# A third buffer for high and low parts, a spread change from the cosine half to the sine half, and one transposition for maxima and sums

## The chip, the cores and the metric

One core of a Trainium2 chip. The metric is the device time of one launch in microseconds, the median of several runs.

## What is computed

Two branches of the same input x (2048 rows of 512, fp32) are mixed by a gate of each row:

```
g = sigmoid((x * gate_w).sum(-1))
a = x @ Wd_re.T ;  b = x @ Wd_im.T              # DFT along the 512 columns
A = Ws_re @ a - Ws_im @ b                       # DFT along the 2048 rows, real part
q, k, v = x @ wqkv                              # 32 heads of 16
p = softmax(mask(q @ k.T / 4))                  # a row sees itself and the 255 rows before it
B = (p @ v) @ wo
out = g * A + (1 - g) * B
```

## The kernel before

**Precision.** Every dense product is made of three matmuls: each fp32 operand is split into a rounded high part and the rest, the low part (`split`, lines 77 to 81, from SBUF; `split_psum`, lines 83 to 88, from PSUM), and `TERMS` (line 223) lists high by high, high by low and low by high.

**Two streams in one order.** TensorE's order is written by hand. The loop at the end of the kernel (from line 710) goes over 128 attention blocks n (4 groups of heads by 32 blocks of 64 rows). In block n it makes four score matmuls (`s_pair`, L324), for which VectorE takes the row maxima (L326, into `nm`) and ScalarE the exponentials' sums (L329, into `l`). For block k = n - 20 it makes four transposed score matmuls (`t_pair`, L393), whose operands hold the negated maxima in four extra rows, and every third block it multiplies probabilities by v (`pv`, L420). Between these, `fill` pulls 3 to 3.6 dense matmuls per quarter block from the generator `dense`, which yields after each matmul. The order of VectorE, ScalarE, GpSimd and SyncE (SP) is decided by a scheduler from simulated times and from what waits for what; `behind(...)` puts an instruction behind the last marked one of an engine. All large transfers but one kind are issued from SP's queue, in order.

**The dense stream** has these stages. First q, k (`qk_proj`, L243) and v (`v_proj`, L265). The q and k blocks leave PSUM through `qk_evict`: ScalarE writes the high part and VectorE the low part of a tile `hl` (4 KB per partition, two buffers), and SP stores it in `qk_scr`. `ring_load` fetches it back into `ring`, from which `make_pad` (L307, L309) builds the padded stationary operands; one quarter of a ring (512 rows) is loaded when its last readers are done, a few blocks ahead of the first `make_pad` that needs it. Then b and a (`ab_proj`, L265): b goes through the same `hl` tiles into `ab_scr`; of a, 12 of the 16 chunks are written straight into tiles `big` (16 buffers), and 4 go through `hl` and `ab_scr`. Beside it the gate is computed (`gate`, L208, with `gwb`, the gate's weights, as a constant tile).

Then comes the joint over the 2048 rows, in two halves: half 0 with the cosine matrix and a, half 1 with the sine matrix and b. A block `tb` (16 per half) accumulates 16 chunks by 3 terms, 48 matmuls (L451), in one PSUM buffer of `ps_d` (two). The matrix comes in pieces of 8 chunks (`c_pieces`), 512 KB each, which VectorE splits. Half 0 stores its blocks, times g, in `r_scr[0]` (`store_r`, L567). Half 1 loads them, adds its own (`add_r`, L588) and stores the sum in `r_scr[1]`; once attention is done, the blocks are combined with the output projection (`wo_block`, L638, L640).

At the change of halves all 16 tiles `big` have to go from a to b. `c_pair` does it: the last two blocks of half 0 run side by side, the second four chunks (`BEHIND`) behind the first, and when both have used a chunk, its tile is loaded with the b chunk. The first two blocks of half 1 run as a pair too.

**Maxima and sums.** Eight blocks after another (16 times in all) the 32 columns of maxima and the 32 columns of sums are transposed on TensorE: `m_rows` (L336) negates and splits the maxima (L339, L340) and stores them in `m_scr`, `l_rows` (L352) takes the reciprocals (L350) before and a copy (L354) after and stores them in `l_scr`. Both come one after the other in the order. `m_ring` fetches the maxima into the ring from ScalarE's queue (L346) one block later. `pv` loads the reciprocals into `rl` (one buffer of the pool `at`) and multiplies (L430).

**Small tiles.** The pool `ev` has five buffers of 2 KB per partition, for v, `store_r`, `add_r` and the output projection.

Of the kernel before, what the change touches and what calls it, by code (L numbers as in the profile page):

```python
# [7 lines left out]
F32 = mybir.dt.float32  # L8
# [19 lines left out]
BEHIND = 4  # L28
# [4 lines left out]
def fnet_window_mix(ctx: ExitStack, tc: tile.TileContext, xT, x, wqk, wv, wr, wi, cr, ci, wo, gw, out):  # L33
# [19 lines left out]
    r_scr = [[dram.tile([P, D], F32, name=f"r_scr{i}_{c}") for c in range(16)] for i in range(2)]  # L53
# [140 lines left out]
    gwb = const.tile([P, D], F32, name="gwb")  # L194
# [3 lines left out]
    def gate_load(j):  # L198
        if j == 0:
            with behind("sp"):  # L200
                ld(gwb, bass.AP(tensor=gw.tensor, offset=gw.offset, ap=[[0, P], [1, D]]))
        GX[j] = st.tile([P, 1024], F32, name="raw", bufs=2)
        for c in range(2):
            ld(GX[j][:, HALVES[c]], x[2 * j + c])

    def gate(tb):
        t = GX[tb // 2][:, HALVES[tb % 2]]
        nc.vector.scalar_tensor_tensor(t, t, 1.0, gwb, op0=OP.mult, op1=OP.mult,  # L208
                                       accum_out=gl[:, tb:tb + 1])
# [74 lines left out]
    def ab_proj(i, sb, w, dst=None):  # L284
        ps = ps_d.tile([P, 512], F32, name="dab", tag="d")
        yield from row_proj(sb, w, ps)
        if dst is None:
            hl = ev.tile([P, 2, 512], F32R, name="hl", bufs=2)
# [43 lines left out]
    def m_rows(u):  # L332
        U = u % 4
        nm = ML[u][0]
        pt = ps_a.tile([P, 512], F32, name="s", tag="st")
        nc.tensor.matmul(pt[:32, :P], nm, ident, start=True, stop=True)  # L336
# [4 lines left out]
        ld(m_scr[u].rearrange("x p (j r) -> (p j) x r", r=64), f(hl[:]).rearrange("c a h r -> c (a h) r"))  # L341

# [4 lines left out]

    def l_rows(u):
        l = ML.pop(u)[1]
        nc.vector.reciprocal(l, l)  # L350
        pt = ps_a.tile([P, 512], F32, name="s", tag="st")
        nc.tensor.matmul(pt[:32, :P], l, ident, start=True, stop=True)  # L352
        lt = at.tile([32, P], F32, name="lt", bufs=1)
        nc.vector.tensor_copy(lt, pt[:32, :P])  # L354
        for a in range(2):
            ls = l_scr[u]
            ld(bass.AP(tensor=ls.tensor, offset=ls.offset + a * 512, ap=[[1024, NP], [64, 8], [1, 64]]),
               lt[:, 64 * a:64 * a + 64])
# [47 lines left out]
    def pv(n):  # L406
# [41 lines left out]
    def c_chunk(w, i, ab, ps):  # L448
        s8 = i % 8
        for a, b in TERMS:  # L450
            nc.tensor.matmul(ps, w[a][:, s8 * 128:(s8 + 1) * 128], ab[SC[i]][:, b],  # L451
                             start=i == 0 and a + b == 0, stop=i == 15 and a == 1)
            if i < 15 or a == 0:
                yield

    def c_block(get, half, tb, ab, done):
        ps = ps_d.tile([P, 512], F32, name="dc", tag="d")
        for i in range(16):
            if i % 8 == 0:
                w = get((half, tb * 2 + i // 8))  # L460
            yield from c_chunk(w, i, ab, ps)
# [3 lines left out]
    def c_pair(get, half, tb, ab, done, last=False):  # L465
        ps = [ps_d.tile([P, 512], F32, name="dc", tag="d") for _ in range(2)]
        w = [None, None]
        for i in range(16 + BEHIND):
            for h in range(2):
                k = i - BEHIND * h  # L470
                if 0 <= k < 16:
                    if k % 8 == 0:
                        w[h] = get((half, 2 * (tb + h) + k // 8))
                    yield from c_chunk(w[h], k, ab, ps[h])
                    if last and h:
                        nxt[SC[k]] = load_ab(1, SC[k])
                    if k == 15:
                        done(tb + h, ps[h])
                        yield
# [13 lines left out]
    def dense():  # L493
# [71 lines left out]
        def store_r(tb, ps):  # L565
# [4 lines left out]
        get = c_pieces([*((0, k) for k in (*range(28), 28, 30, 29, 31)),  # L570
                        *((1, k) for k in (0, 2, 1, 3, *range(4, 32)))])
# [6 lines left out]
        mixed = {}  # L578

        def add_r(tb, ps):  # L580
            r = mixed.pop(tb, None)
            late_r = r is not None
            if not late_r:
                r = ev.tile([P, 512], F32, name="ev")
                ld(r, r_scr[0][tb])
# [9 lines left out]
        yield from c_pair(get, 1, 0, ab, add_r)  # L595
        for tb in range(2, 16):
# [33 lines left out]
    def wo_block(tb, half):  # L630
        o = O.pop(tb)
        r = ev.tile([P, 512], F32, name="ev")
        ld(r, r_scr[half][tb])
# [41 lines left out]
    maxima = sent = 0  # L675
    need(("qk", 0, 0))
# [3 lines left out]
    for n in range(N + LAG + 2):  # L680
# [16 lines left out]
        for p in range(NP):  # L697
# [68 lines left out]
```

## Time and profile before

| | |
|---|---|
| median of 3 runs | 873.6 us (870.97 to 875.23) |
| profiled execution | 873.98 us, of which the span from first to last instruction is 872.2 us |
| TensorE busy | 860.1 us, 5192 matmul instructions |
| VectorE, ScalarE, GpSimd busy | 601.9, 581.4, 387.8 us |
| moved by DMA | 153.70 MB, mean 176 GB/s |

The profile is of one execution. "PE" is TensorE's matmuls, "PEld" its weight loads, DVE is VectorE, ACT ScalarE, POOL GpSimd, SP SyncE; "SPq" is an instruction that SP's queue issues. L451 is line 451 of the kernel before. Matmuls are pipelined, so the duration of one is longer than the step from its start to the next one's start; a step is read from two start times. A name such as dc<-big,hi is the tile written and those read.

### The profile page before, as it was taken

What the parts mean: (1) busy time and instruction counts of PE and PEld (TensorE: products, weight loads), DVE (VectorE), ACT (ScalarE), POOL (GpSimd) and SP (SyncE); (2) the same over time, 40 slices, a digit from 0 to 9 for tenths busy, and PEclk for the clock granted to TensorE, in tenths of its full rate; (3) what the DMA queues carried; (4) which work ended last, traced back from release to release, by engine and by line L of the source; (5) the groups of instructions that cost most, each with busy time, mean ns of one, the idle gap of its engine ahead of it and who ended that gap; (6) DMA issues with size and microseconds to landing.
All of it is one profiled execution on the core that took longest, in us unless ns stands there. A gap on an engine that the chain in (4) does not pass through costs nothing.

```text
span 872.2 us, 17214 instructions
## 1 busy us (share of the span) xinstructions
PE 860.1 (99%) x5192; PEld 693.5 (80%) x5192; DVE 601.9 (69%) x1966; ACT 581.4 (67%) x1793; POOL 387.8 (44%) x1067
## 2 busy tenths in 40 slices
PE   9999999999999999999999999999899999999998
PEld 7888778787878778788787887878678787788886
DVE  4588986667879987778787777878585444564431
ACT  5488799888988888788788877878676454111110
POOL 9100154445536746656465666554466665200000
PEclk9999999999999999999999999999999999999999
DMA  7865686465758537634355353589644332376541
GB/s 244 286 218 172 217 253 191 161 207 174 235 171 262 173 95 222 173 116 154 121 148 151 121 143 122 149 282 293 209 144 139 117 119 103 127 265 191 190 145 49
DMA packets 90829, 153.70 MB, mean 176 GB/s; under 512 B 26864, under 2 KB 35824, under 8 KB 90736
## 3 DMA queue, kind: packets, MB, share of 16 engines
q1 hardware_dynamic: 89984, 151.42, 55.3%
q10 hardware_dynamic: 752, 1.18, 0.4%
q8 instruction: 41, 0.67, 0.3%
q14 instruction: 52, 0.43, 0.2%
HBM read 104.60 MB, written 47.97 MB: 175 GB/s over the span
## 4 chain that ended last, share of the span: by engine, by line
PE 91%; DMA 5%; DVE 2%; ACT 1%; issue 0%; SPq 0%; DVEq 0%; ACTq 0%
PE dc L451 39%; PE dab L265 9%; PE s L324 8%; PE o L420 8%; PE dqk L243 8%; PE t L393 8%; PE dv L265 5%; PE t L638 5%; DMA qk_scr<-hl 2%; DMA ring<-qk_scr 1%; DMA big<-ab_scr 1%; DVE sm L326 1%; DMA pt<-wqk 1%; PE s L231 0%; DVE pad L309 0%
## 5 line engine op out<-in xcount | busy, mean ns | idle before, releaser
L451 PE MATMUL dc<-big,hi 128*128 128x512 f32 x1024 | 356.0, 396 | 0.0
L399 POOL TENSOR_SCALAR_AFFINE_SELECT pt<-pt 64x128 f32<-64x128 f32 x512 | 192.7, 376 | 274.0 <-ACT pt L394 257.7
L329 ACT ACTIVATE sm<-sm,nm 128x320 f32<-128x320 f32 (+4 forms) x512 | 277.9, 544 | 49.4 <-DVE nm L326 47.9
L326 DVE CUSTOM_DVE_ANT_0 sm<-s,mask 128x320 f32<-128x320 f32 (+4 forms) x512 | 231.7, 461 | 95.8 <-PE s L324 75.3
L394 ACT ACTIVATE pt<-t 128x320 f32<-128x320 f32 (+4 forms) x512 | 209.0, 412 | 93.0 <-PE t L393 91.1
L451 PEld LDWEIGHTS dc<-big,hi 128*128 128x128 f32 x1024 | 186.6, 188 | 32.8 <-issue 2.5
L451 PE MATMUL dc<-big,lo 128*128 128x512 f32 x512 | 201.8, 394 | 0.0
L403 POOL TENSOR_SCALAR_AFFINE_SELECT pt<-pt 64x128 f32<-64x128 f32 x448 | 165.6, 370 | 0.0
L324 PE MATMUL s<-ring,pad 128*128 128x320 f32 (+4 forms) x512 | 158.4, 309 | 4.3 <-DVE nm L326 3.9
L393 PE MATMUL t<-ring,pad 128*128 128x320 f32 (+4 forms) x512 | 154.7, 302 | 0.3 <-DVE nm L326 0.3
L309 DVE TENSOR_SCALAR pad<-ring,half 96x256 fp32r<-96x256 f32 x384 | 120.4, 356 | 28.0 <-PE t L393 22.5
L324 PEld LDWEIGHTS s<-ring,pad 128*128 128x128 f32 x512 | 96.1, 188 | 38.6 <-issue 8.5
L393 PEld LDWEIGHTS t<-ring,pad 128*128 128x128 f32 x512 | 96.3, 188 | 18.7 <-DVE nm L326 1.4
L451 PEld LDWEIGHTS dc<-big,lo 128*128 128x128 f32 x512 | 96.4, 188 | 10.8
L81 DVE TENSOR_TENSOR lo<-raw,hi 128x512 fp32r<-128x512 f32 x146 | 98.9, 708 | 1.3 <-PE dc L451 1.3
L329 ACT ACTIVATION_READ_ACCUMULATOR sm<-sm,nm 128x1 f32 x512 | 99.1, 194 | 0.0
L265 PE MATMUL dab<-hi,big 128*128 128x512 f32 x256 | 91.1, 396 | 0.9 <-DVE hl L88 0.9
L243 PE MATMUL dqk<-big,hi 128*128 128x512 f32 x240 | 86.6, 394 | 1.1 <-DVE hl L86 0.5
L80 DVE CAST hi<-raw 128x512 fp32r<-128x512 f32 x142 | 59.0, 456 | 37.8 <-PE dc L451 36.3
L420 PE MATMUL o<-pt,vpad 128*32 128x320 f32 (+4 forms) x1408 | 74.4, 353 | 0.0
L383 POOL COPY vpad<-vr 64x256 f32<-64x256 f32 x64 | 26.0, 407 | 91.3 <-DMA vr<-v_scr 71.6
L307 ACT ACTIVATE pad<-ring,half 96x256 fp32r<-96x256 f32 x128 | 64.2, 502 | 0.0
(83 smaller groups left out, 777.3 us busy)
## 6 DMA issues: line engine op xcount, KB each, us to landing
qk_scr<-hl SPq DMA_DIRECT2D x32, 512.0 KB
ring<-qk_scr SPq DMA_DIRECT2D x32, 512.0 KB
raw<-cr SPq DMA_DIRECT2D x32, 512.0 KB
raw<-ci SPq DMA_DIRECT2D x32, 512.0 KB
ab_scr<-hl SPq DMA_DIRECT2D x20, 512.0 KB
big<-ab_scr SPq DMA_DIRECT2D x20, 512.0 KB
ring<-qk_scr SPq DMA_DIRECT2D x32, 256.0 KB
r_scr<-ev SPq DMA_DIRECT2D x28, 256.0 KB
```

The source lines that it names most:

```text
L243: nc.tensor.matmul(ps, w[a][:, c:c + 128], XT[dk, ss][:, b], start=n == 0, stop=n == 11)
L265: nc.tensor.matmul(ps, XT[dk, ss][:, a, c * 128:(c + 1) * 128], wh[b], start=n == 0, stop=n == 11)
L309: nc.vector.tensor_scalar(dst, src, half[:96, h:h + 1], None, op0=OP.mult)
L324: nc.tensor.matmul(ps[:, :w], PAD[0, n][:, p], ring[1][:, p, k0:k0 + w], start=True, stop=True)
L326: mark("dve", nc.vector.tensor_tensor_reduce(out=sm[:, :w], in0=ps[:, :w], in1=mask[:, WIN - w:], scale=1.0, scalar=3e38, op0=OP.add, op1= ...
L329: mark("act", nc.scalar.activation(sm[:, :w], sm[:, :w], AF.Exp, bias=nm[:, c], scale=-1.0, accum_out=l[:, c]))
L393: nc.tensor.matmul(ps[:, :w], PAD[1, n][:, p], ring[0][:, p, q0:q0 + w], start=True, stop=True)
L394: nc.scalar.activation(pt[:, p, :w], ps[:, :w], AF.Exp, scale=-1.0)
L399: nc.gpsimd.affine_select(a, a, pattern=[[0, 2], [1, 64]], compare_op=OP.is_ge, fill=0.0, base=0, channel_multiplier=-1)
L403: nc.gpsimd.affine_select(a, a, pattern=[[0, 2], [-1, 64]], compare_op=OP.is_gt, fill=0.0, base=0, channel_multiplier=1)
L420: nc.tensor.matmul(OT[g, sb][32 * p:32 * p + 32, q - sb * 512:e - sb * 512], v2[:, p], pt[:, p, q - q0:e - q0], start=first, stop=kb == 8 ...
L451: nc.tensor.matmul(ps, w[a][:, s8 * 128:(s8 + 1) * 128], ab[SC[i]][:, b], start=i == 0 and a + b == 0, stop=i == 15 and a == 1)
```

## The change

- `hl` has three buffers. To make room, three tiles of 2 KB per partition go into `ev`: `rl`, the gate's weights `gwb`, and the zero operand of the first matmuls. The two tiles of maxima and sums become one tile `ml`.
- `m_rows` and `l_rows` become `ml_rows`: the reciprocals are taken first, one matmul transposes all 64 columns, VectorE reads the maxima from rows 0 to 31 and the reciprocals from rows 32 to 63 of its result. `m_ring` comes at least two blocks after it.
- `c_pair` goes. The last four blocks of half 0 and the first four of half 1 (`SWITCH`) are cut in halves of 8 chunks (`c_half`): first the lower chunks of all four, then the upper chunks of all four. Each half is an accumulation of its own in PSUM; the parts are added through `r_scr`, with a third set `r_scr[2]`: a lower part is stored, and the upper part loads it, adds and stores. In the four upper halves of half 0 two b chunks each are loaded into the tiles of the lower chunks, in the four lower halves of half 1 two each into those of the upper chunks.

```diff
-BEHIND = 4
+SWITCH = 4
...
-    r_scr = [[dram.tile([P, D], F32, name=f"r_scr{i}_{c}") for c in range(16)] for i in range(2)]
+    r_scr = [[dram.tile([P, D], F32, name=f"r_scr{i}_{c}") for c in range(16)] for i in range(3)]
...
-        zero = at.tile([P, 512], F32R, name="rl", bufs=1)
+        zero = ev.tile([P, 512], F32R, name="ev")
...
-    gwb = const.tile([P, D], F32, name="gwb")
+    gwb = []
...
+            gwb.append(ev.tile([P, D], F32, name="ev"))
...
-        hl = ev.tile([P, 2, 512], F32R, name="hl", bufs=2)
+        hl = ev.tile([P, 2, 512], F32R, name="hl", bufs=3)
...
-            ML[u] = [at.tile([P, NP * 8], F32, name="nm"), at.tile([P, NP * 8], F32, name="l")]
-        nm, l = ML[u]
+            ML[u] = at.tile([P, 2, NP * 8], F32, name="ml")
+        nm, l = ML[u][:, 0], ML[u][:, 1]
...
-    def m_rows(u):
-        U = u % 4
-        nm = ML[u][0]
+    def ml_rows(u):
+        ml = ML.pop(u)
+        nc.vector.reciprocal(ml[:, 1], ml[:, 1])
         pt = ps_a.tile([P, 512], F32, name="s", tag="st")
-        nc.tensor.matmul(pt[:32, :P], nm, ident, start=True, stop=True)
+        nc.tensor.matmul(pt[:64, :P], ml.rearrange("p x c -> p (x c)"), ident, start=True, stop=True)
...
+        lt = at.tile([64, P], F32, name="lt", bufs=1)
+        nc.vector.tensor_copy(lt[32:64], pt[32:64, :P])
...
-    def l_rows(u):
...
-            rl = at.tile([P, 512], F32, name="rl", bufs=1)
+            rl = ev.tile([P, 512], F32, name="ev")
...
+    def c_half(get, half, tb, j, ab, done, after=None):
+        ps = ps_d.tile([P, 512], F32, name="dc", tag="d")
+        w = get((half, tb * 2 + j))
+        r = done[0](tb)
+        for c in range(2):
+            if after:
+                after()
+            k = 8 * j + 4 * c
+            yield from c_part(w, range(16)[k:k + 4], ab, ps, (8 * j, 8 * j + 7))
+            if c == 0:
+                yield
+        done[1](tb, ps, r)
+        yield
...
+        def add(src, dst, after=None):
+            def load(tb):
+                r = ev.tile([P, 512], F32, name="ev")
+                with behind("sp"):
+                    ld(r, src(tb))
+                return r
+
+            def done(tb, ps, r):
+                nc.vector.scalar_tensor_tensor(r, ps, g1[:, tb:tb + 1], r, op0=OP.mult, op1=OP.add)
+                ld(dst(tb), r)
+                if after:
+                    after(tb)
+            return load, done
...
+        def next_b():
+            sc = todo_b.pop(0)
+            with behind("sp"):
+                nxt[sc] = load_ab(1, sc)
...
-        for tb in range(14):
+        for tb in range(16 - SWITCH):
             yield from c_block(get, 0, tb, ab, store_r)
-        yield from c_pair(get, 0, 14, ab, store_r, True)
+        for j in range(2):
+            for tb in lasts:
+                yield from c_half(get, 0, tb, j, ab,
+                                  (lambda t: None, lambda t, ps, r: store_r(t, ps)) if j == 0 else
+                                  add(lambda t: r_scr[0][t], lambda t: r_scr[2][t]),
+                                  next_b if j else None)
...
-        yield from c_pair(get, 1, 0, ab, add_r)
-        for tb in range(2, 16):
+        for j in range(2):
+            for tb in first:
+                yield from c_half(get, 1, tb, j, ab, add(r_in, lambda t: r_scr[2][t]) if j == 0 else
+                                  add(lambda t: r_scr[2][t], lambda t: r_scr[1][t], wait.append),
+                                  None if j else next_b)
+        for tb in range(SWITCH, 16):
...
-            if p == 2 and sent < maxima:
+            if p == 2 and sent < maxima and n >= taken[sent] + 2:
                 m_ring(sent)
                 sent += 1
...
-                    m_rows(maxima)
-                    l_rows(maxima)
+                    ml_rows(maxima)
                     maxima += 1
+                    taken.append(n)
```

More of the change, by code (lines that the diff above doesn't have):

```diff
@@ L346, in m_ring @@
             nc.scalar.dma_start(f(ring[0][96:100, :, U * 512:(U + 1) * 512]), m_scr[u])
-    def l_rows(u):
[L349 to L358, printed above, removed]
     OT = {}
@@ L446, in fnet_window_mix, with c_part @@
     SC = [*range(4, 16), *range(4)]
[L448 to L454, printed above, removed]
+    def c_part(w, chunks, ab, ps, ends):
+        for i in chunks:
+            for a, b in TERMS:
+                nc.tensor.matmul(ps, w[a][:, i % 8 * 128:i % 8 * 128 + 128], ab[SC[i]][:, b],
+                                 start=i == ends[0] and a + b == 0, stop=i == ends[1] and a == 1)
+                if i != chunks[-1] or a == 0:
+                    yield
     def c_block(get, half, tb, ab, done):
         ps = ps_d.tile([P, 512], F32, name="dc", tag="d")
[L458 to L461, printed above, removed]
+        for j in range(2):
+            yield from c_part(get((half, tb * 2 + j)), range(16)[8 * j:8 * j + 8], ab, ps, (0, 15))
+            if j == 0:
+                yield
         done(tb, ps)
         yield
[L465 to L479, printed above, removed]
+    def c_half(get, half, tb, j, ab, done, after=None):
[8 more added lines that the diff above has]
+            if c == 0:
+                yield
+        done[1](tb, ps, r)
+        yield
     have = set()
@@ L578, in dense, with r_in @@
         mixed = {}
+        def r_in(tb):
+            return r_scr[2 if tb in lasts else 0][tb]
         def add_r(tb, ps):
@@ L632, in wo_block @@
         r = ev.tile([P, 512], F32, name="ev")
-        ld(r, r_scr[half][tb])
+        ld(r, r_scr[half if half or tb < 16 - SWITCH else 2][tb])
         ps = ps_a.tile([P, 512], F32, name="t", tag="st")
@@ L675, in fnet_window_mix @@
     maxima = sent = 0
+    taken = []
     need(("qk", 0, 0))
```

21 lines of the change are left out of this document (15 added, 6 removed).

## The prediction

> **What bounds the kernel now.** I read the busy times first, then TensorE's waits, then the windows, then the chain of work around each wait. The page's first part says who is busy:
>
> ```profile
> PE 860.1 (99%) x5192; PEld 693.5 (80%) x5192; DVE 601.9 (69%) x1966; ACT 581.4 (67%) x1793; POOL 387.8 (44%) x1067
> ```
>
> TensorE is busy for 860.1 of 872.2 us, so the time can fall in three ways only: fewer or shorter matmuls, less of the 12.1 us of idling, or less time at a lowered clock. TensorE's own waits, longest first, begin with
>
> ```profile
> PE s L324 <- DVE nm L326: 3.9, 2, 2.8
> ```
>
> (3.9 us in 2 waits, the longest 2.8). The view of the windows shows where that is. Its columns are: busy us of PE, PEld, DVE, ACT, POOL (and instructions), granted clock, share of the DMA engines, GB/s.
>
> ```profile
> 80.00:100.00 20.00, 18.74 (x90) 15.33 (x90) 16.42 (x65) 14.75 (x47) 0.81 (x2) 1.00 0.82 234
> 100.00:120.00 20.00, 19.59 (x93) 15.41 (x91) 18.38 (x65) 17.86 (x56) 8.64 (x22) 1.00 0.85 265
> ...
> 280.00:300.00 20.00, 20.00 (x114) 15.80 (x113) 18.90 (x69) 17.98 (x57) 12.42 (x31) 1.00 0.49 145
> 300.00:320.00 20.00, 19.36 (x136) 15.78 (x136) 16.59 (x62) 17.90 (x58) 11.22 (x33) 1.00 0.49 137
> ...
> 560.00:580.00 20.00, 20.00 (x123) 16.26 (x123) 15.03 (x53) 16.46 (x53) 12.64 (x34) 1.00 0.77 216
> 580.00:600.00 20.00, 20.00 (x119) 16.08 (x118) 17.18 (x62) 16.07 (x59) 6.97 (x20) 1.00 0.97 323
> 600.00:620.00 20.00, 17.16 (x108) 13.24 (x111) 10.75 (x40) 13.53 (x42) 8.60 (x30) 0.91 1.05 318
> 620.00:640.00 20.00, 20.00 (x143) 16.06 (x136) 17.05 (x55) 14.11 (x44) 12.20 (x28) 1.00 0.40 132
> ```
>
> The reader is to see one bad window, 600 to 620: 2.84 us without TensorE, a mean clock of 0.91, and DMA engines that have been full since 580. That is the change of halves. The chain there runs over one transfer, and VectorE stands for it:
>
> ```profile
> 601.90 12.84 DMA ring<-qk_scr
> ```
>
> ```profile
> 614.84 0.87 DVE L309 TENSOR_SCALAR pad<-ring,half 96x256 fp32r<-96x256 f32 x3 [3.65 <-DMA ring<-qk_scr]
> ```
>
> The last part of a ring for attention waits among the b chunks and lands 12.84 us after issue; VectorE can't build the padded operand, nor take the maxima queued behind it, so no PSUM buffer for scores comes free and TensorE stops.
>
> **The change of halves.** TensorE's timeline gives the price:
>
> ```profile
> 612.71 0.40 PE L451 MATMUL dc<-big,hi 128*128 128x512 f32 x1
> 612.94 0.40 PE L451 MATMUL dc<-big,lo 128*128 128x512 f32 x1
> 616.17 0.45 PE L324 MATMUL s<-ring,pad 128*128 128x320 f32 x1 [2.84 <-DVE nm L326]
> 616.42 1.05 PE L451 MATMUL dc<-big,hi 128*128 128x512 f32 x2
> ```
>
> From start to start 3.23 us pass where the step before took 0.23, so 3.0 us are lost. Then the clock: 0.09 of 20 us is 1.8 us. Together **4.8 us**.
>
> Does the stall go? In the changed order of SP's queue, between the two ring1 transfers and this ring0 transfer stand one b chunk (0.5 MB), one matrix piece (0.5), three r_scr transfers (0.26 each) and a v part (0.06): 1.8 MB. Before, there were six b chunks, one piece, one r_scr store and two v parts: 3.9 MB. At the 318 GB/s of the full window, 2.1 MB less is 6.6 us earlier, and VectorE waited 3.65 us. So the stall goes with some 3 us to spare. I take the whole 4.8 us.
>
> What the change adds here: eight more additions on VectorE (one for each of the eight blocks that now come in two parts), with eight loads and eight stores of 0.26 MB. One addition takes 741 ns:
>
> ```profile
> L588 DVE SCALAR_TENSOR_TENSOR ev<-dc,g,ev 128x512 f32<-128x512 f32 x15 | 11.1, 741 | 3.7 <-PE dc L451 3.7
> ```
>
> The matmuls stay the same in number. The spread takes 16 half blocks of 24; the eight with b loads hold 192 matmuls, and this window of L451 alone (PE busy, count) holds 59 in 20 us:
>
> ```profile
> 560.00:580.00 20.00, 18.06 (x59) 9.79 (x58) 1.00 0.77 216
> ```
>
> so they last 65 us, with 8 x 0.741 = 5.9 us more of VectorE, or 1.8 us per 20. The window 620 to 640 would come to 18.9 us, just what 280 to 300 had with TensorE at 20.00; the next one, 300 to 320, had 0.64 us of idling. I charge **0.6 us** once; the ends are 0 and 2.6 (0.64 in each of four windows). Each addition waits in VectorE's order for its part's last matmul, with maxima, padded operands and splits queued behind it, and TensorE waits for the maxima; that is where such 0.64 would come from. A part is loaded a half block ahead (24 of 59 matmuls in 20 us: 8 us), and PSUM has a second buffer, so neither is late by itself. On SP's queue the loads wait for a free `ev` buffer, with ring parts and pieces behind them; these have the margin above.
>
> **The third buffer.** The chain of work from 76 to 121 us shows two stores that ScalarE waited for:
>
> ```profile
> 88.05 6.06 DMA qk_scr<-hl
> 94.19 0.61 ACT hl L84
> ...
> 112.38 7.11 DMA qk_scr<-hl
> 119.51 0.61 ACT hl L84
> ```
>
> A store of `hl` landed 6.06 and 7.11 us after issue, and with two buffers the next high part stood for it, with exponentials behind it. On TensorE:
>
> ```profile
> 94.54 0.38 PE L352 MATMUL s<-ident,l 128*32 128x128 f32 x2
> 95.98 0.41 PE L324 MATMUL s<-ring,pad 128*128 128x320 f32 x1 [1.05 <-DVE nm L326]
> ...
> 118.48 0.31 PE L393 MATMUL t<-ring,pad 128*128 128x320 f32 x1
> 118.63 0.63 PE L265 MATMUL dab<-hi,big 128*128 128x512 f32 x2
> ...
> 119.70 0.31 PE L393 MATMUL t<-ring,pad 128*128 128x320 f32 x1
> 120.89 0.50 PE L265 MATMUL dab<-hi,big 128*128 128x512 f32 x1 [0.88 <-DVE hl L88]
> ```
>
> The first step is 1.44 us instead of 0.31 (below, 586.13 to 586.44), the second 1.19 instead of 0.15. Lost: 1.1 + 1.0, **2.1 us**. With three buffers a part waits for the store of the third one before it, not of the second. What is late next is VectorE, at 18.38 of 20 us; if it were as late as ScalarE was, nothing would be won (0). But in the first wait it idled for ScalarE itself:
>
> ```profile
> 94.83 0.69 DVE L88 SCALAR_TENSOR_TENSOR hl<-dqk,hl 128x512 fp32r<-128x512 f32 x1 [2.04 <-ACT hl L84]
> ```
>
> So I take the full 2.1.
>
> The tiles moved into `ev` (reciprocals, gate weights) hold buffers longer. In the changed order up to three of five are held while a is made, when no other tile of `ev` is in use. I charge nothing; if a store of a finished block had to wait for one, the second PSUM buffer would cover a block of 48 matmuls, 16 us.
>
> **The merged transposition.** One of the 16 places:
>
> ```profile
> 585.91 0.38 PE L336 MATMUL s<-ident,nm 128*32 128x128 f32 x2
> 586.13 0.38 PE L352 MATMUL s<-ident,l 128*32 128x128 f32 x2
> 586.44 0.41 PE L324 MATMUL s<-ring,pad 128*128 128x320 f32 x1
> ```
>
> Each transposition takes 0.22 us from start to start and streams the same 128 columns whether 32 or 64 columns stand in the array. One of two goes: 16 x 0.22 = **3.5 us**. It now waits for the reciprocal, as the second one did before; VectorE's work is the same in number. The later `m_ring` moves one small transfer in ScalarE's order by about ten instructions; TensorE doesn't wait there now, so 0.
>
> A weight load's length depends on its columns:
>
> ```profile
> L451 PEld LDWEIGHTS dc<-big,lo 128*128 128x128 f32 x512 | 96.4, 188 | 10.8
> ...
> L336 PEld LDWEIGHTS s<-ident,nm 128*32 128x32 f32 x32 | 3.2, 110 | 1.3 <-issue 0.7
> ```
>
> (188 - 110) / 96 = 0.81 ns a column, so 32 columns more take 26 ns more; if a load isn't hidden, 2 x 16 x 0.026 = 0.8 us of the 3.5 goes (rival 4). I take 0, because loads lie beside matmuls elsewhere: PE is busy for 99% and PEld for 80% of the same span.
>
> The Trainium skill, "TensorE: Matmul & The Clock Gate" (Part 3, The mechanism), speaks for rival 4: a weight load overlaps with a matmul in flight only where the two use different groups of rows of the array, and these use the same ones. By that rule the sum would be 865.0, without it 864.2. The trace so far speaks against the rule, by the 99% and 80%.
>
> **Sum**, against the profiled execution's 873.98: 873.98 - 4.8 - 2.1 - 3.5 + 0.6 = 864.2. The median shown is 873.6, 0.4 lower, within the runs' spread.
>
> **Rivals.**
> 1. The ring part is late all the same. For it: DMA stays near full. The shares of the four windows from 560 make 63.8 of 80 us; 16 transfers of 0.26 MB at 0.318 MB per us add 13 us, so 77 of 80. Against it: 6.6 us earlier against 3.65 needed. Then the 4.8 us stay: 869.0.
> 2. The third buffer doesn't help, because VectorE was as late: 866.3.
> 3. Slower: the DMA engines become the bound over the whole spread. From the point where its transfers take more than the 80 us (3 us above the estimate), b chunks or parts come late and TensorE stands for them. The price is at most the 13 us added, with the stall kept: 864.2 + 13 + 4.8 = 882. Against it: the b chunk with the least time is asked for 33 matmuls, 11 us, before its use.
> 4. The wider weight load of the transposition shows: 865.0.
>
> **How the numbers follow.** Forecast (863 to 866): 0.54. Rival 4: 0.10. Rival 2: 0.10. Rival 1: 0.16, half of it with a little more lost, above 869.6. Rival 3: 0.10, of which 0.07 above 878.4. The range goes from 861.5 (no cost on VectorE, 863.6, less 2.1 of the 2.6 us by which the lowest run lies under the median) to 869.5, which takes in rival 1's 869.0; 0.18 are left out. A difference of 0.5% (4.4 us) is about what can be told from no change: faster 0.54 + 0.10 + 0.10 + 0.08 = 0.82, within 0.08 + 0.03 = 0.11, slower 0.07.
>
> **What would show it.** After: no wait of TensorE over 1 us and a clock of 1.00 from 560 to 640; the ring0 transfer there landing in under 9 us; no ScalarE wait on qk_scr<-hl; one transposition of 128*64 with a step of 0.22 us, 5160 matmul instructions; VectorE near 18.9 of 20 us at the change of halves. A new wait of TensorE for big<-ab_scr, or for VectorE behind the additions in parts, would make the prediction wrong.

## The result and the profile after

The kernel after takes **870.66 us** (median of 22 executions, 869.63 to 873.62), the kernel before 873.58 (22 executions, 870.39 to 878.6). The ratio is 0.9974 (95% interval 0.9961 to 0.9986): 2.3 us faster by the ratio and 2.9 by the medians, where 9.8 were forecast, and the time lies above the range. The profiled execution of the kernel after took 873.39 us (span 871.3), one of the slowest of the 22.

The page's first part, and TensorE's waits (us in total, times, longest):

```profile
PE 860.5 (99%) x5160; PEld 690.3 (79%) x5160; DVE 611.3 (70%) x1974; ACT 580.9 (67%) x1793; POOL 384.6 (44%) x1067
```

```profile
PE s L232 <- DVE big L80: 2.0, 1, 2.0
PE dv L484 <- DVE ev L129: 1.5, 1, 1.5
PE t L388 <- DVE ml L327: 0.9, 3, 0.4
PE dqk L244 <- DVE hl L86: 0.5, 1, 0.5
PE t L388 <- ACT pad L308: 0.5, 1, 0.5
PE s L325 <- DVE ml L327: 0.5, 2, 0.3
```

The 2.8 us wait is gone, and no wait of scores for maxima is over 0.3. The longest wait, 2.0, is new and stands at the very start. TensorE is busy for as long as before with 32 matmuls fewer. The windows, with the columns that they had in the prediction:

```profile
80.00:100.00 20.00, 19.94 (x96) 16.39 (x95) 17.55 (x70) 16.42 (x52) 0.79 (x2) 1.00 0.78 234
100.00:120.00 20.00, 19.25 (x91) 15.27 (x90) 18.64 (x67) 17.46 (x56) 4.96 (x13) 1.00 0.89 232
280.00:300.00 20.00, 19.88 (x113) 15.64 (x114) 19.33 (x71) 18.19 (x57) 13.36 (x34) 1.00 0.50 155
...
560.00:580.00 20.00, 19.80 (x119) 15.12 (x117) 15.70 (x52) 15.40 (x50) 11.95 (x33) 1.00 0.99 305
580.00:600.00 20.00, 20.00 (x117) 15.95 (x117) 17.58 (x64) 15.42 (x56) 6.75 (x20) 1.00 0.90 304
600.00:620.00 20.00, 19.74 (x133) 15.44 (x132) 17.86 (x56) 15.87 (x50) 11.98 (x32) 1.00 1.05 317
```

600 to 620 has 19.74 instead of 17.16 and a clock of 1.00 instead of 0.91: in this profile the change of halves did what was forecast. 80 to 100 is nearly full, but 100 to 120 idles for 0.75, and 560 to 580 idles where it did not before. Of the signs that the prediction named, three came: no wait of TensorE over 1 us and a clock of 1.00 from 560 to 640, no wait of ScalarE for a store of q or k, and 5160 matmul instructions. VectorE was at 17.86 of 20 us at most, below the 18.9. The part of a ring at the change of halves landed 10.6 us after its issue at 600.35, not in under 9, which was early enough all the same; and the step of the one transposition is not 0.22, as shown below.

**Where the time went, by place.** The pv matmuls come in 43 groups, the same in every kernel here. How much later a group starts than the same group in the profile of before is called the shift below; its growth over a stretch is what that stretch cost (plus) or won (minus). The table gives it in us (stretches in times of before; "to the end" and the total go to the end of the last matmul). Each row is one profiled execution; the kernels below the first three rows are those of the experiments.

| kernel | to 122.5 | to 260.3 | to 290.2 | to 569.2 | to 600.0 | to 650.4 | to the end | total |
|---|---|---|---|---|---|---|---|---|
| after | +1.04 | -0.20 | +1.12 | -0.26 | +1.22 | -3.76 | -0.10 | -0.94 |
| after, again | -1.24 | -0.28 | +0.73 | -0.27 | +1.04 | -3.78 | -0.10 | -3.90 |
| before, again | -0.29 | +0.00 | -0.01 | +0.08 | +0.00 | +2.08 | +0.04 | +1.90 |
| spread change alone | -0.25 | -0.04 | -0.02 | +0.02 | +0.39 | -4.21 | +0.00 | -4.11 |
| third buffer alone | -2.65 | -0.10 | +1.60 | +0.50 | +0.01 | +0.59 | -0.00 | -0.05 |
| moved tiles alone | -0.92 | -0.02 | +3.29 | +0.02 | +0.01 | -0.19 | -0.00 | +2.19 |
| merged transposition alone | +3.00 | +1.02 | +0.65 | -0.29 | +1.01 | -3.02 | -0.10 | +2.27 |
| old transpositions in after | -2.35 | -0.08 | +3.20 | +1.08 | +2.60 | -4.24 | +0.00 | +0.21 |
| transposition ahead of pv | -2.04 | +0.09 | +1.06 | -0.33 | +2.10 | -4.23 | -0.22 | -3.57 |
| side by side | -2.79 | +0.18 | +1.37 | -1.50 | +0.26 | -3.34 | +0.72 | -5.10 |
| old order, side by side | -2.56 | -0.72 | -0.25 | -1.47 | -0.18 | -3.62 | +0.73 | -8.07 |
| old order, side by side, again | -2.54 | -0.65 | +0.23 | -1.49 | -0.13 | -2.31 | +0.73 | -6.16 |

Four things stand out for the kernel after. The +1.04 of the first stretch holds 3.07 us from the first 12 us, of which the second profile has 0.2. The change of halves gives -3.8, but 1.0 to 1.2 come back just ahead of it, near 571. Near 278 another 0.7 to 1.1 go. And between 290 and 569, where nothing but the transposition changed, seven of the 16 places give 0.26 together, not 7 x 0.22 = 1.5.

The two new waits, in VectorE's and SP's timelines of the kernel after:

```profile
277.64 0.69 DVE L209 SCALAR_TENSOR_TENSOR raw<-raw,ev 128x512 f32<-128x512 f32 x1 [0.91 <-DMA raw<-x]
278.71 0.69 DVE L209 SCALAR_TENSOR_TENSOR raw<-raw,ev 128x512 f32<-128x512 f32 x1 [0.37 <-DMA raw<-x]
...
573.95 0.69 DVE L425 TENSOR_TENSOR ev<-o,ev 128x512 f32<-128x512 f32 x1 [3.14 <-DMA ev<-l_scr]
```

```profile
260.88 0.42 SPq L56 DMA_DIRECT2D ev<-gw  x1
261.36 1.90 SPq L56 DMA_DIRECT2D ev<-l_scr  x2
...
565.95 0.63 SPq L56 DMA_DIRECT2D ev<-l_scr  x1
```

Near both are loads of the reciprocals, whose tile moved into `ev`. Two of them (0.26 MB each) now go out 10 us ahead of the gate's rows (`raw<-x`); later a third goes out at 565.95 and lands 8 us after, while VectorE stands for it from 570.8.

The theory after this result: (a) the spread change and the third buffer give about what was forecast; (b) the merged transposition saves next to nothing; (c) the moved reciprocals cost 2 us that the prediction did not charge. The rival to (c): the transfers do not fit there, whoever owns the buffer.

### The profile page after: what moved, and what is told of

The parts are those of the page before. It is cut to its first block, busy times and chain, and to the rows that moved or that the text cites. A ratio compares the mean times of both kernels' runs of the same rounds, so it can differ in the third digit from the quotient of the medians.

```text
span 871.3 us, 17146 instructions
## 1 busy us (share of the span) xinstructions
PE 860.5 (99%) x5160; PEld 690.3 (79%) x5160; DVE 611.3 (70%) x1974; ACT 580.9 (67%) x1793; POOL 384.6 (44%) x1067
## 3 DMA queue, kind: packets, MB, share of 16 engines
q10 hardware_dynamic: 752, 1.18, 0.4%
## 4 chain that ended last, share of the span: by engine, by line
PE 92%; DVE 3%; DMA 2%; ACT 1%; issue 1%; SPq 0%; DVEq 0%; ACTq 0%
PE dc L446 40%; PE dab L266 9%; PE s L325 8%; PE o L415 8%; PE dqk L244 8%; PE t L388 8%; PE t L669 5%; PE dv L266 4%; DVE sm L327 1%; PE s L232 1%; DMA raw<-x 1%; ACT sm L330 1%; DMA ring<-qk_scr 1%; PE s L337 1%; DMA pt<-xT 0%
## 5 line engine op out<-in xcount | busy, mean ns | idle before, releaser
L394 POOL TENSOR_SCALAR_AFFINE_SELECT pt<-pt 64x128 f32<-64x128 f32 x512 | 191.9, 375 | 276.4 <-ACT pt L389 261.2
L330 ACT ACTIVATE sm<-sm,ml 128x320 f32<-128x320 f32 (+4 forms) x512 | 277.3, 543 | 49.4 <-DVE ml L327 48.0
L398 POOL TENSOR_SCALAR_AFFINE_SELECT pt<-pt 64x128 f32<-64x128 f32 x448 | 161.9, 361 | 0.1
L446 PEld LDWEIGHTS dc<-big,lo 128*128 128x128 f32 x512 | 96.3, 188 | 10.6
L330 ACT ACTIVATION_READ_ACCUMULATOR sm<-sm,ml 128x1 f32 x512 | 98.8, 193 | 0.0
```

Of the source, the lines that this page charges most:

```text
L330: mark("act", nc.scalar.activation(sm[:, :w], sm[:, :w], AF.Exp, bias=nm[:, c], scale=-1.0, accum_out=l[:, c]))
L394: nc.gpsimd.affine_select(a, a, pattern=[[0, 2], [1, 64]], compare_op=OP.is_ge, fill=0.0, base=0, channel_multiplier=-1)
L398: nc.gpsimd.affine_select(a, a, pattern=[[0, 2], [-1, 64]], compare_op=OP.is_gt, fill=0.0, base=0, channel_multiplier=1)
L446: nc.tensor.matmul(ps, w[a][:, i % 8 * 128:i % 8 * 128 + 128], ab[SC[i]][:, b], start=i == ends[0] and a + b == 0, stop=i == ends[1] and a ...
```

## The experiments

### The parts one by one, on the kernel before

The merged transposition alone (`m_rows` and `l_rows` become `ml_rows`, as in the change), the third buffer alone (`hl` with 3 buffers; `rl`, `gwb` and `zero` in `ev`), the spread change alone (`rl` keeps its buffer), and the moved tiles alone:

```diff
-            rl = at.tile([P, 512], F32, name="rl", bufs=1)
+            rl = ev.tile([P, 512], F32, name="ev")
```

and the same for `gwb` and `zero`, with two buffers for `hl`.

> The kernel before with the merged transposition alone (and the later ring transfer that goes with it). Theory 1, from the traces of before and after: a place loses only 0.06 us (the step from the last pv matmul to the transposition grows by 0.11 us, and the step behind it is 0.36 instead of 0.31), and 0.19 us at the two places with no pv ahead: 14 x 0.06 + 2 x 0.19 = 1.2 us, so a change of -1.2 us, with the grown steps at the same 14 places. Theory 2, the prediction's sum: 16 x 0.22 = -3.5 us; then the 0.11 us in the kernel after came from its neighbours and is absent here.

> The kernel before with the third buffer for high and low parts alone, with the reciprocals, the gate's weights and the zeros in the shared pool to make room. Theory 1: the two waits for stores of high parts go (-2.1 us), some 0.9 us comes back at the first place as waits for padded operands, and the two early loads of reciprocals hold up the gate's rows by 1.15 us near 278 us: -2.1 + 0.9 + 1.15, about 0 (-0.5 to 0.3). Theory 2, the prediction: -2.1 us, with no wait near 278.

> The kernel before with the spread change of halves alone; the reciprocals keep their own buffer. Theory 1: the late load of reciprocals (VectorE stands 3.14 us for it near 571 in the kernel after) comes from the shared pool, so it is absent here, and the change gives what the prediction took, -4.8 + 0.6 = -4.2 us (-3.8 to -4.6). Theory 2: the load is late because the DMA engines are full (0.99 to 1.05 of their time from 560 to 620 in the kernel after), whoever owns its buffer: then VectorE stands for it here too and the change is -2.5 to -3 us.

> The kernel before with only the reciprocals, the gate's weights and the zeros moved into the shared pool; two buffers for high and low parts as before. Theory 1: reciprocals are now loaded as early as a buffer is free, two of them (0.26 MB each) beside the gate's rows, and VectorE waits for those near 278 us: +1.15 us. Theory 2, the prediction: nothing (0).

Measured, against the kernel before (873.91): merged 872.59, ratio 0.9994 (0.9981 to 1.0007); third buffer 875.16, 1.0012 (0.9996 to 1.0027); spread 871.83, 0.998 (0.9965 to 0.9995); moved tiles 875.71, 1.0023 (1.0003 to 1.0043).

The spread change shows its -4.2 at its place. Its reciprocals go out 42.6 us ahead of their use, and VectorE stands only for TensorE (SP's and VectorE's timelines):

```profile
526.76 0.63 SPq L56 DMA_DIRECT2D rl<-l_scr  x1
```

```profile
569.32 0.69 DVE L430 TENSOR_TENSOR rl<-o,rl 128x512 f32<-128x512 f32 x1 [0.51 <-PE o L420]
```

Timed, the spread change gives 1.7 us (0.4 to 3.1), less than its one profile. The granted clock of each execution shows a part of why. A window at 0.91 lowers the mean of an execution to 0.998, and of the 35 executions of the kernel before 11 have 0.999 or more (median 872.4 us): they lack the lowered clock that the prediction charged. Of the 12 with the spread change 4 still have less than 0.999 (median 874.2 us); its profile is one of the other eight, so where these stall is not shown.

The moved tiles cost 2 us, timed and in the trace. The place is 260 to 290, and the chain is one that no theory had: the small store of maxima is issued behind the two early loads and has landed only at 268.7; ScalarE stands for it to issue `m_ring` (at 267.03 in the kernel before), and the exponentials behind that are late. ScalarE, TensorE and SP in the kernel with the moved tiles alone:

```profile
268.76 0.64 ACTq L347 DMA_DIRECT2D ring<-m_scr  x1
269.44 0.22 ACT L395 ACTIVATE pt<-t 128x64 f32<-128x64 f32 x1 [2.72 <-DMA m_scr<-mhl]
```

```profile
269.72 0.41 PE L394 MATMUL t<-ring,pad 128*128 128x320 f32 x1 [1.18 <-ACT pt L395]
270.98 0.42 PE L325 MATMUL s<-ring,pad 128*128 128x320 f32 x1 [0.39 <-ACT pt L395]
```

```profile
259.58 2.04 SPq L56 DMA_DIRECT2D ev<-l_scr  x2
261.72 0.65 SPq L56 DMA_DIRECT2D l_scr<-lt  x1
262.47 0.60 SPq L56 DMA_DIRECT2D m_scr<-mhl  x1
```

Third buffer less moved tiles is -0.05 - 2.19 = -2.2 us, of which -2.65 + 0.92 = -1.7 lie in the first stretch, where the two waits for stores are gone. So in the profiles the buffer by itself gives about what was forecast, and the room made for it costs as much; timed, the two kernels differ by 0.5 us, which their intervals do not tell from nothing.

The merged transposition alone moves SP's order too: near 122 ScalarE stands 3.52 us for a store of high parts, and at the change of halves TensorE waits 0.88 instead of 2.84. A queue planned anew moves such waits about, so this kernel's total says little, its places more. One place speaks against (c) for the wait near 278: here VectorE waits for the gate's rows too, with the reciprocals in a buffer of their own, and the moved tiles alone have no such wait.

```profile
280.50 0.83 DVE L208 SCALAR_TENSOR_TENSOR raw<-raw,gwb 128x512 f32<-128x512 f32 x1 [0.59 <-DMA raw<-x]
```

In the kernel before these rows land at 275.0 and VectorE takes them at 275.8 (the trace's times), so little is needed to make them late. That the wait near 278 in the kernel after comes from the moved tiles is not shown.

### What a transposition costs

In the kernel before, a place looks like this (start, duration; the pv group, the two transpositions, scores). Each transposition is two matmul instructions (x2), which I call its two passes.

```profile
383.97 1.83 PE L420 MATMUL o<-pt,vpad 128*32 128x320 f32 x40
385.62 0.38 PE L336 MATMUL s<-ident,nm 128*32 128x128 f32 x2
385.84 0.38 PE L352 MATMUL s<-ident,l 128*32 128x128 f32 x2
386.15 0.41 PE L324 MATMUL s<-ring,pad 128*128 128x320 f32 x1
```

And in the kernel after, below it a pv group with no transposition behind it:

```profile
385.87 1.83 PE L415 MATMUL o<-pt,vpad 128*32 128x320 f32 x40
387.63 0.43 PE L337 MATMUL s<-ident,ml 128*64 128x128 f32 x2
387.99 0.41 PE L325 MATMUL s<-ring,pad 128*128 128x320 f32 x1
...
570.93 1.83 PE L415 MATMUL o<-pt,vpad 128*32 128x64 f32 x32
572.69 0.41 PE L325 MATMUL s<-ring,pad 128*128 128x320 f32 x1
```

From the pv group to scores: 2.18 us with two transpositions, 2.12 with the merged one, 1.76 with none. So the two cost 0.42 and the merged one 0.36. Two kernels ask why: one has the transposition ahead of pv, the other has it split into two matmuls in neighbouring groups of 32 columns of the array.

```diff
+                if maxima < 16 and n > 8 * maxima + 8:
+                    ml_rows(maxima)
...
                 for j in range(k - 3, k):
```

```diff
-        nc.tensor.matmul(pt[:64, :P], ml.rearrange("p x c -> p (x c)"), ident, start=True, stop=True)
+        for x in range(2):
+            nc.tensor.matmul(pt[32 * x:32 * x + 32, :P], ml[:, x], ident, start=True, stop=True)
```

> The kernel after with the merged transposition ahead of the pv matmuls instead of behind them. Theory 1: a weight load of 64 columns or more can't be hidden behind pv matmuls (in both kernels the time from the first pv matmul to what follows is 1.76 us before scores and before the merged transposition, but 1.65 us before the old 32-column one), so the merged one pays those 0.11 us and scores behind it pay again for a load (0.36). Ahead of pv it stands between loads of 128 columns: the transposition adds about 0.22 to 0.25 us, pv follows it with 32 columns, and one 1.76 remains: 0.33 + 0.25 + 1.76 = 2.34 us from the matmul ahead to scores, against 0.33 + 1.76 + 0.36 = 2.45; 14 x 0.11 = 1.5 us less than the kernel after. Theory 2: the transposition is dear by itself (two passes, 64 columns), wherever it stands: 2.45 us or more, no change or up to 1 us slower.

> The kernel after, with the merged transposition split again into two matmuls of 32 columns, the second into the next 32 columns of the array and rows of PSUM. Theory 1: the first takes 1.65 us from the first pv matmul as before; if matmuls in different groups of columns run side by side the second costs under 0.1 us instead of 0.22, and 1.65 + 0.1 + 0.31 = 2.06 against 1.76 + 0.36 = 2.12 now, 14 x 0.06 = 0.8 us less. Theory 2: they run one after the other: 1.65 + 0.22 + 0.31 = 2.18 as before the change, 0.8 us more than the kernel after.

> The kernel after with the transposition as two matmuls of 32 columns in neighbouring groups of columns, timed this time. From its trace (1.65 us from the first pv matmul to the transpositions and 0.32 from there to scores, 1.97 against 2.12 us): 14 x 0.15 = 2.1 us less than the kernel after if nothing is given back, 868.5; the trace gave back 0.7 us between 693 and 734, so 868.5 to 869.3. The rival: waits near 278 and 571 take all of it, 870.5.

Ahead of pv: 870.55 us, 0.9961 (0.9941 to 0.9981), no different from the kernel after. From the matmul ahead to scores are 2.45 us here (382.64 to 385.09) and 0.33 + 2.12 there:

```profile
382.64 0.40 PE L446 MATMUL dc<-big,hi 128*128 128x512 f32 x1
382.97 0.43 PE L337 MATMUL s<-ident,ml 128*64 128x128 f32 x2
383.33 1.83 PE L415 MATMUL o<-pt,vpad 128*32 128x320 f32 x40
385.09 0.41 PE L325 MATMUL s<-ring,pad 128*128 128x320 f32 x1
```

It costs its 0.36 wherever it stands; theory 1 falls, theory 2 holds. Side by side:

```profile
382.35 1.83 PE L416 MATMUL o<-pt,vpad 128*32 128x320 f32 x40
384.00 0.39 PE L338 MATMUL s<-ident,ml 128*32 128x128 f32 x4
384.31 0.41 PE L325 MATMUL s<-ring,pad 128*128 128x320 f32 x1
```

Both start at 384.00 and scores follow 0.31 later, as behind a single one: 1.96 us, so the pair costs 0.20 instead of 0.36. Theory 1 holds, with more than twice its size (0.15 us against the merged one, not 0.06). It took 869.09 us once and 868.57 timed, 0.9944 (0.9909 to 0.9979). From 690 to 734 all kernels with this edit give 0.7 us back. There is no wait there and the clock is 1.00; the steps of the dense matmuls and the transposed scores are on average some 3 ns longer, and why stays open.

> The kernel after once more, with a profile. Theory 1: the 2.0 us that TensorE stood at the start for the first rows of x (3.06 us of shift within 30 us) were chance of that one execution; here the start is that of before and the span about 868.3. Theory 2: the moved zeros delay the start: 3 us again.

> The kernel after with the two old transpositions (and the earlier ring transfer that went with them): third buffer and spread change alone. Theory 1: a place costs 0.06 us more, 0.8 us in all for 14, and ScalarE waits again for maxima on their way to the ring near 268 us, because its transfer stands behind the two loads of reciprocals: +1.5 to 2 us there. Theory 2: each place costs 0.22 us more, 3.5 us in all.

The kernel after once more took 870.22 us, without the wait at the start: it does not come in every execution. The side-by-side kernel had it in one of its two profiles:

```profile
7.33 0.47 PE L232 MATMUL s<-big,hi 128*128 128x512 f32 x1 [2.02 <-DVE big L80]
```

With the old transpositions the kernel after takes 874.76 us (once). Its +3.20 to 290 is ScalarE's wait for the store of maxima again, so the later ring transfer, which the prediction put at nothing, is worth some 2 us beside the moved tiles. Between 290 and 569 the 1.08 lies at one place near 360.

### Which order the reciprocals' loads need

First, reciprocals from the fourth block on in a buffer of `hl`:

```diff
+            rl = (ev.tile([P, 2, 512], F32, name="hl", bufs=3)[:, 0] if ("ab", 3) in have else
+                  ev.tile([P, 512], F32, name="ev"))
```

Second, those of the last eight blocks in `hl`, and the first eight issued behind everything written before them:

```diff
+            with behind(*(("sp",) if u < 8 else ())):
```

Last, the old order, each load behind the store of the block before, and the last eight in `hl`:

```diff
-            rl = ev.tile([P, 512], F32, name="ev")
+            rl = (ev.tile([P, 2, 512], F32, name="hl", bufs=3)[:, 0] if g >= 2 else
+                  ev.tile([P, 512], F32, name="ev"))
...
-            ld(rl, bass.AP(tensor=ls.tensor, offset=ls.offset, ap=[[512, 2 * NP], [0, 16], [1, 512]]))
+            with behind("rl"):
+                ld(rl, bass.AP(tensor=ls.tensor, offset=ls.offset, ap=[[512, 2 * NP], [0, 16], [1, 512]]))
...
             ld(o_scr[sb][g], rl)
+            last["rl"] = last["sp"]
```

> The kernel after, with the reciprocals from the fourth block on in a buffer of the high and low parts, which no one else uses by then, instead of the shared pool of five. Theory 1: the load that VectorE stood for (3.14 us, 570.8 to 573.95) was late because its buffer came free late and its issue stood behind parts, and the gate's rows were late (waits of 0.91 and 0.37 us near 278) because two loads of reciprocals went ahead of them; both go: 1.3 + 1.1 = 2.4 us less than the kernel after, about 868.3. Theory 2: the DMA engines are full there and only the order of who is late changes: the wait near 571 stays or another as long takes its place; within 0.5 us of the kernel after.

> The kernel after with the loads of reciprocals ordered as in the other kernel (the first eight behind the transfers written before them, the last eight in a buffer of the high and low parts), and nothing else. Theory 1: two loads of reciprocals of 0.26 MB that go out ahead of the gate's rows make these late; without them the shift between 276 and 290 us falls from +0.7 to +1.5 us to under 0.3, and the one between 569 and 584 from 1.1 to under 0.2. Theory 2: the gate's rows are late for another reason (the stores of high parts, which now come in a denser row): the shift near 278 stays.

> The kernel after, in which each load of reciprocals is issued only behind the store of the block before it, as a buffer of their own made them do; the first eight stay in the shared pool, the last eight use a buffer of the high and low parts. Theory 1: what the own buffer gave was this order; with it the shift between 276 and 290 us is under 0.3 instead of 0.7 to 1.5, that between 569 and 584 under 0.2 instead of 1.1, and no other wait of VectorE for these loads appears: 1.5 to 2.4 us less than the kernel after, 868.3 to 869. Theory 2: the transfers don't fit beside the third buffer's denser stores; one of the two waits stays or shows again elsewhere, and the kernel is within 0.7 us of the kernel after.

> The kernel after with the old order of the loads of reciprocals, profiled once more. Theory 1: the gate's rows land within a few tenths of the time at which VectorE asks for them, so chance decides in each execution; the shift between 276 and 290 us differs from the 1.26 of the first profile by over 0.5. Theory 2: it belongs to this kernel's order of transfers: 1.0 to 1.5 us again.

The `hl` buffer: 873.14 us, 0.9998 (0.9978 to 1.0018). The wait near 571 goes (-0.04), but the one near 278 grows to +3.89: a load of reciprocals now goes out at 266.99, right ahead of the gate's rows at 267.91, and the first two of them land 7.2 and 8.3 us after issue instead of 4.8 and 5.1 in the kernel before. Behind everything: 871.92 us once; the gate's rows are in time, but VectorE stands for the reciprocals themselves (+1.66 to 260, +0.87 to 290). The old order: 868.23 us, 0.9925 (0.9902 to 0.9948), 2.4 us less than the kernel after by the medians. Near 571 nothing is left in either profile (-0.04), as theory 1 says; but the `hl` buffer alone did that too, with the load issued 101 us ahead of its use, so that a buffer outside the pool is enough there, and what the order adds was not tried by itself. Near 278 the shift was +1.26 and then -0.02 in the same kernel. So it differs from one execution to the next, and the order seems to move the odds: +0.73 to +3.2 in every profile with the third buffer and freely ordered loads in `ev`, -0.25 to +1.26 in four with the old order.

### The kernels put together

> The kernel after with two edits: the transposition as two matmuls of 32 columns in neighbouring groups of columns (it gained about 0.15 us a place), and the loads of reciprocals ordered: the first eight stay in the shared pool but are issued behind the transfers written before them, the last eight use a buffer of the high and low parts. Theory 1: the gate's rows come in time near 278 (0.7 to 1.5 us), VectorE doesn't stand for reciprocals near 571 (1.1 us), and the transpositions give 16 x 0.15 = 2.4 us: some 4.2 to 5 us less than the kernel after, 865 to 866.5. Theory 2: the order of transfers only moves the waits about: the transpositions' gain alone, 868 to 869.

> The kernel before with the spread change of halves and the transposition as two matmuls of 32 columns in neighbouring groups of columns; two buffers for high and low parts, and nothing moved into the shared pool. Theory 1: -4.1 (the spread change alone) and 16 x 0.2 = -3.2 us, about 866.4, with no wait near 278; the third buffer's 2.2 us are missing. Theory 2: the two waits for stores of high parts near 96 and 122 us grow, as with the merged transposition alone in the kernel before (+4 us there): about 870.

> The same order of loads, and the transposition as two matmuls of 32 columns in neighbouring groups of columns. Theory 1: 0.15 us a place for 14 places (2.1 us) and 1.5 to 2.4 us less than the kernel after: 866 to 867, and shifts under 0.3 us at 276 to 290 and at 569 to 584. Theory 2: 868 to 869, no better than the two transpositions alone.

> The old order of loads with the side-by-side transpositions, profiled once more. Theory 1 (chance): a shift of 0.5 us or more between 276 and 290 in this profile, or none again; the two profiles of the other kernel differ too. Theory 2 (the kernel): under 0.2 us again, and 864 to 866 us in the span.

> The kernel before, profiled once more. Theory 1: nothing but the start and a few tenths differ from the first profile: the two waits for stores of high parts near 96 and 121 us, no wait near 278, and the 3.0 us at the change of halves come again. Theory 2: these waits are chance too, and one of them is gone or doubled here; then the gains that the experiments found from one profile each are worth that much less.

The first is the side-by-side kernel with the second order of loads: 869.21 us, 0.9951 (0.9933 to 0.997), near theory 2, which gave it the transpositions' gain alone; its loads are late as above. The second (the spread change and the side-by-side transpositions on the kernel before) took 869.77, 0.9962 (0.9947 to 0.9976); it has no wait near 278, and TensorE waits 1.28 and 0.70 us for low parts of VectorE near 104 and 121. The third, the kernel after with the old order and side by side, took **866.35 us, 0.9903 (0.9871 to 0.9936)**, and 867.98 once more: faster than both kernels. TensorE's waits in its first profile:

```profile
PE dv L488 <- DVE ev L129: 1.5, 1, 1.5
PE dqk L244 <- DVE hl L88: 0.7, 1, 0.7
PE dqk L244 <- DVE hl L86: 0.5, 1, 0.5
PE s L325 <- DVE ml L327: 0.5, 2, 0.3
```

In its second profile a piece of the sine matrix is late after the change of halves, for VectorE and then for TensorE:

```profile
620.59 0.86 DVE L80 CAST hi<-raw 128x512 fp32r<-128x512 f32 x2 [1.71 <-DMA raw<-ci]
```

```profile
622.56 0.42 PE L389 MATMUL t<-ring,pad 128*128 128x320 f32 x1 [0.68 <-DVE ml L327]
```

Four of the 15 profiles with the spread change, this one among them, lose 0.6 to 1.3 us there; all four have reciprocals in `hl`, as have three others that lose none.

The kernel before once more (875.87 us) shows the same waits at the same places, but the stall at the change of halves is 4.17 instead of 2.84:

```profile
618.27 0.64 PE L324 MATMUL s<-ring,pad 128*128 128x320 f32 x1 [4.17 <-DVE nm L326]
```

A profile of one execution prices such a wait to 1 or 2 us, no better.

## Why the prediction was wrong

- **Change of halves, -4.8 + 0.6.** The mechanism was right: no stall, clock 1.00, -4.11 in the profile alone, and some 0.4 given back between 584 and 600. For the median the term was too large: timed alone it gave 1.7 us. I priced the stall and its clock from one execution, and 11 of 35 executions of the kernel before do not have that clock, while 4 of 12 with the change alone still have a lowered clock, no profile shows where.
- **Third buffer, -2.1.** The mechanism was right: in the 14 profiles with the buffer no wait of ScalarE for such a store is over 0.4 us. The size, -2.2, is the difference of two single profiles, and the times do not confirm it. In the kernel after, a wait of 0.5 for a padded operand on ScalarE shows near 106 in its place.
- **The moved tiles, "I charge nothing".** A step that failed: its price was put at nothing. I asked whether a finished block's store would find a buffer, and covered that with PSUM. What changed was the order of the loads: with a buffer of its own a load waited for the store before it, in the shared pool it goes out as soon as any buffer is free (two at 261, ahead of the gate's rows) or, among parts and b chunks, only 4.9 us ahead of its use instead of 42.6. Alone this cost 2.2 us in the profile and 2.0 timed. In the kernel after it cost 1.0 to 1.2 near 571, which comes only where the spread change and the moved tiles come together. The 0.7 to 1.1 near 278 may be its doing only in part, since the merged transposition alone had +0.65 there.
- **Merged transposition, 16 x 0.22 = -3.5.** The other step that failed. I took the step between two starts, 0.22, as the price of one and of the merged one. The two passes of the narrow one start 0.109 us apart, which makes that 0.22. The two of the wide one start 0.160 apart, and ahead of it the pv group takes 0.11 longer than ahead of a narrow one. 14 x 0.06 and 2 x 0.19 at the places without pv make -1.2. Rival 4 had the direction and 0.8 of the 2.3 us that were lost. Why the wide pass is so much dearer is not shown. By my estimate 128 columns stream in a quarter of the 0.23 us that 512 take, 0.057. With the narrow load of 110 ns that makes 0.17 a pass, one after the other, and with the wide one of 134 ns 0.19; both passes are shorter, so both hide something, and the wide one less. The rule of the Trainium skill, "TensorE: Matmul & The Clock Gate" (Part 3, The mechanism), that a load is hidden only behind matmuls in other groups of rows, would hide nothing in either, and the trace does not bear it out. My argument against it, 99% and 80% of the span, was no price for the transposition either: it is an average mostly over loads of 188 ns beside matmuls of 512 columns, whose step of 0.23 us covers one.
- **Later ring transfer, 0.** It hides a wait of some 2 us that the moved tiles would have made.

With the prices of single profiles: 873.98 - 4.1 - 2.2 + 2.2 - 1.2 = 868.7, and 869.8 with the wait near 571; 870.22 and 870.66 were measured. With the timed ratios of the parts (0.998, 1.0012 and 0.9994) the sum is 1.2 us less than before, against 2.3 measured; each of these is known to 1.1 to 1.4 us either way, so the times neither confirm this split nor contradict it. Rivals 1 and 3 did not come in the kernel after: DMA was at 0.99 and 1.05 of its time, and no b chunk was late. The late piece of the sine matrix in four other profiles is rival 3 at a small part of its price.

## What to carry to other kernels

A tile that moves from a buffer of its own into a shared pool loses the order that the single buffer gave its loads: write that order down again, find it a buffer that nobody else wants, or charge the loads at the busiest place that they can move to. A stall that was read from one execution is not yet the median's: look at how many executions have it. The price of a small matmul is the time from the one ahead to the one behind, with it and without it, not the step between two alike. Two narrow matmuls in different groups of columns cost less here than one that is wider.

## What the runs showed of the hardware

- Two 32-column transpositions in neighbouring groups of columns start together and cost 0.20 us; in the same group they cost 0.42, and one of 64 columns costs 0.36. The Trainium skill, "TensorE: Matmul & The Clock Gate" (Part 3, Measured speedup vs the span model), tells of such a gain from packing by columns; the trace agrees.
- A pv group of 32-column matmuls takes 1.65 us up to a following 32-column matmul and 1.76 up to a wider one: 0.11 us that the first transposition of the kernel before had saved unseen.
- The first rows of x kept TensorE waiting for 2.0 us in 2 of the 20 profiles, one of them the first of the kernel after, which makes 3 us of shift. Both are among the 15 with the zeros in `ev`, so whether the change moves the odds is not shown.
- Whether a stall lowers the clock is not told by its length alone: the stretch of 20 us has a granted clock of 0.91 around a wait of 2.0 us (after, 0 to 20) and around one of 1.18 (moved tiles alone, 260 to 280), and 1.00 around one of 2.12 (old transpositions in after, 260 to 280).
